# Attention and two dense layers fused on one core: the second layer's first three token blocks cut into two parts of four steps

## The chip, the core and the metric

The kernel runs on one core of one Trainium2 chip. The core has five engines with a queue of instructions each: PE (TensorE, matrix products; PEld is its weight load), DVE (VectorE), ACT (ScalarE), POOL (GpSimd) and SP (SyncE, which here only issues DMAs). An instruction waits for others by semaphores, and what stands behind it in its engine's queue waits with it. The metric is the device time of one execution in microseconds (us).

## The reference

```python
p_packed = sm_attn(p, k, v)              # 8 batches, 8 heads, 576 tokens, 32 packed queries
attn = sm_attn(q, p_packed, p_packed)    # -> x: 4608 tokens x 512
h = x @ w_in;   y = (h - tanh(h)) @ w_out        # layer 1, 512 -> 2048 -> 512
h = y @ w2_in;  out = (h * cos(h)) @ w2_out      # layer 2, the same sizes
```

All inputs are float64, the output is float32. The kernel keeps near float32 precision by splitting an operand into a high part (float32r) and the rest, and by summing three products of the parts.

## The kernel before, in words

**Weights.** `w2_in` and `w2_out` each come as 16 tiles of 128 x 512 in float64 words. A conversion (`Conv`) of one tile takes three stages: `a` is an ACT copy of the upper word, `b` are three DVE operations on the integer words (shift L144, sign L149, low bits L154), and `c` is an ACT copy to the high part (L177) with a POOL subtraction for the rest (L178). Each finished tile is also stored to memory for later reloading (`store_w2`). The order is w2_in 0, w2_out 0, w2_in 1, and so on; 32 conversions in all.

**Layer 1** runs 128 steps (16 half batches of tokens by 8 steps of 256 hidden units). During its last 16 steps, `STEP_A2` says how many conversions of layer 2 weights are begun in each; the three DVE operations of a conversion then stand between the five of the next step (`el2`).

**Layer 2** goes over nine blocks of 512 tokens. The first three (`NCL = 3`) are done directly, 8 steps each, 24 in all; they are numbered 0 to 23 here. One step s of such a block is: `h2` (24 matmuls, hidden units 256 s and on), `el_cos` and `chunks` of the step before (24 matmuls that add to the four y sums in PSUM). `el_cos` is a chain over two engines: round (ACT L599), fraction (DVE L602), sine and square (ACT L608, L609), product (DVE L612), high part gh (ACT L618), rest gl (DVE L621). PE needs gh of step n for `chunks` of step n, which stands behind `h2` of step n + 1. After a block's last step `evac` copies each of the four sums out and stores it.

In the first block each `el_cos` takes up to three conversions between its operations (`each("ca")`, `each("b")`). The next block's y comes in four pieces, `loady` (a DMA) and `splity` (ACT copy L565, POOL subtraction L566), one piece a step. In the third block two more things are prepared:

- `combine(F)` for F = 0 to 7 makes the weight sums that the later blocks use: two POOL operations on halves of w2_in tiles into `cw` (L670, L673), four POOL operations into `cs` (L681), then an ACT copy (`ws`, L683) and a DVE subtraction (`ws`, L684), and two stores. `COMBINE` gives the steps: 16, 16, 17, 17, 18, 18, 19, 20.
- `bprep` makes the y sums for the first pair of later blocks: 40 small pieces, loads of y (L736), DVE subtractions (L723, L730) and ACT copies (L720). It begins at the sixth step of the third block (`BPREP = 5`, step 21) and its pieces are spread evenly over the steps left.

**The other six blocks** are done in three pairs with fewer products (lines 1050 and on, matmuls L762), weights reloaded from memory. Their first products write PSUM that the direct blocks' h used, so they wait until the last step's product (L612) has read it.

**Order.** From step 15 of layer 1 on the order is that of the program text (`tc.manual_schedule`): every engine works its queue off in the order in which the code emits the instructions, and a pool slot is taken again in the order in which it was given back. Nothing reorders around a wait.

The steps of layer 2 before:

```python
h2(s, yt, st)
el_cos(st, t == 0, (t, s) == (0, 0))
...                       # splity, loady of the next block
    pend += chunks(ht, hs, hst)
...
store_w2()
if t == NCL - 1:
    for F in COMBINE[s]:
        combine(F)
```

Of the kernel before, what the change touches and what calls it, by code (L numbers as in the profile page):

```python
# [10 lines left out]
F32 = mybir.dt.float32  # L11
F32R = mybir.dt.float32r
# [22 lines left out]
PRE_A = (0, 1, 1, 1, 1, 0, 1, 1, 1, 0, 1, 1, 0, 0, 0)  # L35
PRE_B = (1, 0, 1, 1, 2, 0, 2, 2, 0, 1, 2, 2, 0, 3, 0)
STEP_A = (1, 2, 2, 2, 1, 2, 1, 1, 1, 1, 0, 2, 1, 1, 1, 1, 1, 1, 0, 3, 1, 1)
STEP_A2 = (1, 1, 1, 1, 1, 1, 1, 1, 1, 1, 1, 1, 1, 0, 0, 0)
STEP_ORDERED = 15
ATT1 = ((-2, 0, 1, 4), (0, 1, 2, 5))  # L40
ATT = ((0, 2, 3, 8), (1, 4, 5, 10))
# [2 lines left out]
PACK1, PACK = 3, 7  # L44
G0, G1, G = (0, 14, 12), (7, 8, 22, 25), (9, 11, 13, 15)
YLOAD, Y2LOAD, Y2SPLIT = 2, 118, 125
NCL, BPREP, COMBINE = 3, 5, ((0, 1), (2, 3), (4, 5), (6,), (7,), (), (), ())
SGN = -2147483648


# [1 line left out]
def fused_kernel(ctx, tc, qT, kT, v, pT, w1i, w1o, w2i, w2o, ident, out):  # L52
# [502 lines left out]
    def loady(t, k):  # L555
        yr = p2r.tile([128, TB], F32, tag="yr", bufs=2, name="yr")
        nc.sync.dma_start(out=yr, in_=y1[k, :, t * TB:t * TB + TB])
        return yr

    def splity(t, yr, eng):  # L560
        if t % 2 == 0:
# [23 lines left out]
        return p2.tile([128, 2, TB], dt, tag=tag, bufs=2, name=tag)  # L585

    def el_cos(st, cv, cut):
        def each(fns):
            if cv:
                for fn in fns:  # L590
                    getattr(conv2, fn)()

        h = st["h"]
        a = p2.tile([128, 2, TB], F32, tag="a", bufs=1, name="a")
        gh, gl = pt2("gh", F32R), pt2("gl", F32R)
        st["gh"], st["gl"] = gh, gl
# [3 lines left out]
        each("ca")  # L600
# [5 lines left out]
        each("b")  # L606
# [3 lines left out]
        each("ca")  # L610
# [5 lines left out]
        each("b")  # L616
        for x in parts:
            nc.scalar.activation(out=gh[:, x], in_=a[:, x], func=AF.Copy)  # L618
        each("ca")
# [4 lines left out]
        each("b")  # L624

    def chunks(t, s, st):
        def part(jobs):
            if s == 0 and t not in yps:
                yps[t] = [psy.tile([128, DM], F32, tag="y", name="y") for _ in range(4)]
            for m, lo in jobs:  # L630
                for x in range(2):
                    w = st["wo"][x]
                    for wh, gg in ((0, "gl"),) if lo else ((0, "gh"), (1, "gh")):
                        nc.tensor.matmul(  # L634
                            out=yps[t][m], lhsT=st[gg][:, x, 128 * m:128 * m + 128],
                            rhs=w[:, wh, :],
                            start=(s == 0 and x == 0 and not lo and wh == 0),
                            stop=(s == NSTEP - 1 and x == 1 and lo),
                        )
# [11 lines left out]
    def evac(t, m):  # L651
        if m < 2:
            o = p2.tile([128, DM], F32, tag="o", bufs=2, name="o")
        else:
            o = p2x["r"].tile([128, DM], F32, tag="wt", bufs=2, name="o")
        if m % 2 == 0:
            nc.scalar.activation(out=o, in_=yps[t][m], func=AF.Copy, scale=-TWO_PI)
        else:
            nc.vector.tensor_scalar(
                out=o, in0=yps[t][m], scalar1=-TWO_PI, scalar2=None, op0=ALU.mult  # L660
            )
# [343 lines left out]
    pend, hist, bo = [], [], {}
    for t in range(NCL):
        nyt = []
        for s in range(NSTEP):
            st = {}
            h2(s, yt, st)  # L1010
            el_cos(st, t == 0, (t, s) == (0, 0))
            if t + 1 < NCL:
                if 2 <= s < 6:
                    nyt.append(splity(t + 1, yr, nc.gpsimd))
                if 1 <= s < 5:
                    yr = loady(t + 1, s - 1)
            if hist:
                ht, hs, hst = hist.pop(0)
                conv2.need(w2out, 2 * hs + 1)
                hst["wo"] = [w2out[2 * hs + x] for x in range(2)]  # L1020
                pend += chunks(ht, hs, hst)
                n = 1 if (t, s) == (NCL - 1, NSTEP - 1) else len(pend)
                for fn in pend[:n]:
                    fn()
                pend = pend[n:]
            hist.append((t, s, st))
            store_w2()
            if t == NCL - 1:
                for F in COMBINE[s]:
                    combine(F)  # L1030
                if s == BPREP:
                    prep = bprep(NCL, bo)
                if s >= BPREP:
                    n = -(-len(prep) // (NSTEP - s))
                    for fn in prep[:n]:
                        fn()
                    prep = prep[n:]
        yt = nyt
# [162 lines left out]
```

## Time and profile before

| | us |
|---|---|
| median of 3 runs | 1578.78 (1578.52 to 1579.58) |
| the profiled execution | 1577.37 |
| its span, first to last instruction | 1575.5 |
| PE busy | 1491.6 (95%) |
| DVE busy | 1170.5 (74%) |
| ACT busy | 897.3 (57%) |
| POOL busy | 227.2 (14%) |

What lies outside the span is 1.9 us. In time, layer 1 ends at about 800 us of the span, the three direct blocks of layer 2 run from 800 to 1063 us, and the pairs from 1071 us to the end. PE's share of busy time is an average: the stretches in which it idles are few, and each has another cause. The profile's slices show PE at 8 tenths instead of 9 in the two slices before 788 us and at about 1063 us.

### The profile page before, as it was taken

What the parts mean: (1) busy time and instruction counts of PE and PEld (TensorE: products, weight loads), DVE (VectorE), ACT (ScalarE), POOL (GpSimd) and SP (SyncE); (2) the same over time, 40 slices, a digit from 0 to 9 for tenths busy, and PEclk for the clock granted to TensorE, in tenths of its full rate; (3) what the DMA queues carried; (4) which work ended last, traced back from release to release, by engine and by line L of the source; (5) the groups of instructions that cost most, each with busy time, mean ns of one, the idle gap of its engine ahead of it and who ended that gap; (6) DMA issues with size and microseconds to landing.
All of it is one profiled execution on the core that took longest, in us unless ns stands there. A gap on an engine that the chain in (4) does not pass through costs nothing.

```text
span 1575.5 us, 25882 instructions
## 1 busy us (share of the span) xinstructions
PE 1491.6 (95%) x10192; PEld 1293.6 (82%) x10192; DVE 1170.5 (74%) x1596; ACT 897.3 (57%) x1377; POOL 227.2 (14%) x178
## 2 busy tenths in 40 slices
PE   4789999999999999998899999998999999999999
PEld 1568888999999999998877788876888888888887
DVE  6999988787878788789979633567767477747661
ACT  4768655575666666667666543555555354535541
POOL 3632110010101010011314204720000000000000
PEclk9989999999999999999999999999999999999999
DMA  9422322111111111115647310426757474647542
GB/s 348 153 97 98 100 86 91 41 56 46 50 61 65 61 65 46 47 41 176 181 144 272 144 50 0 177 108 223 263 204 269 141 284 161 261 155 281 184 170 111
DMA packets 85050, 217.25 MB, mean 138 GB/s; under 512 B 8576, under 2 KB 36224, under 8 KB 84928
## 3 DMA queue, kind: packets, MB, share of 16 engines
q1 hardware_dynamic: 84928, 215.58, 38.9%
q8 instruction: 81, 1.33, 0.3%
q14 instruction: 41, 0.34, 0.1%
HBM read 169.15 MB, written 46.40 MB: 137 GB/s over the span
## 4 chain that ended last, share of the span: by engine, by line
PE 74%; DVE 15%; issue 4%; ACT 4%; POOL 2%; DMA 1%; SPq 0%; DVEq 0%; POOLq 0%; ACTq 0%
PE y L634 21%; PE y L513 20%; PE p L762 15%; PE h L451 10%; PE h L577 4%; DVE wt L144 2%; PE gp L413 2%; DVE wt L154 2%; DVE wt L149 2%; DVE y L481 1%; DVE t L478 1%; DVE d L479 1%; POOL cs L681 1%; PE pp L320 1%; DVE y L485 1%
## 5 line engine op out<-in xcount | busy, mean ns | idle before, releaser
L513 PE MATMUL y<-gh,w1o 128*128 128x288 f32 x2048 | 308.8, 302 | 16.9 <-ACT gh L493 11.9
L513 PEld LDWEIGHTS y<-gh,w1o 128*128 128x128 f32 x2048 | 281.6, 189 | 46.0 <-ACT t L466 14.9
L762 PE MATMUL p<-b,wa 128*128 128x512 f32 x1008 | 242.2, 391 | 7.6 <-DVE a L612 7.6
L451 PE MATMUL h<-a,g 128*128 128x288 f32 x1536 | 229.7, 299 | 14.6 <-ACT w1i L132 7.1
L451 PEld LDWEIGHTS h<-a,g 128*128 128x128 f32 x1536 | 214.1, 191 | 19.0 <-ACT w1i L132 8.0
L762 PEld LDWEIGHTS p<-b,wa 128*128 128x128 f32 x1008 | 190.5, 189 | 47.8 <-issue 8.0
L466 ACT ACTIVATE t<-h 128x576 f32<-128x576 f32 x128 | 83.3, 651 | 204.7 <-PE h L451 204.5
L634 PE MATMUL y<-wo,gh 128*128 128x512 f32 x768 | 188.1, 389 | 0.0
L634 PEld LDWEIGHTS y<-wo,gh 128*128 128x128 f32 x768 | 144.1, 188 | 30.0
L513 PE MATMUL y<-gl,w1o 128*128 128x288 f32 x1024 | 159.8, 298 | 1.2 <-DVE gl L498 1.2
L513 PEld LDWEIGHTS y<-gl,w1o 128*128 128x128 f32 x1024 | 144.9, 191 | 1.5 <-DVE gl L498 1.4
L577 PE MATMUL h<-yhl,w2i 128*128 128x512 f32 x576 | 134.3, 389 | 0.0
L478 DVE TENSOR_TENSOR t<-h,t 128x576 f32<-128x576 f32 x128 | 95.2, 744 | 52.4 <-ACT u L467 52.0
L485 DVE COPY_PREDICATED y<-k,t 128x576 f32<-128x576 int16 x128 | 118.4, 925 | 11.6
L577 PEld LDWEIGHTS h<-yhl,w2i 128*128 128x128 f32 x576 | 108.1, 188 | 22.4
L493 ACT ACTIVATE gh<-y 128x576 fp32r<-128x576 f32 x128 | 87.6, 684 | 37.5 <-DVE y L485 35.7
L498 DVE TENSOR_TENSOR gl<-y,gh 128x576 fp32r<-128x576 f32 x128 | 102.8, 803 | 6.8 <-ACT gh L493 6.6
L773 ACT ACTIVATE a<-ha 128x1024 f32<-128x1024 f32 x24 | 25.5, 1063 | 140.7 <-DVE ha L770 140.7
L634 PE MATMUL y<-w2o,gh 128*128 128x512 f32 x384 | 93.8, 392 | 8.2 <-ACT gh L618 8.2
L481 DVE SCALAR_TENSOR_TENSOR y<-y,d 128x576 f32<-128x576 f32 x128 | 101.4, 792 | 0.1
L634 PE MATMUL y<-wo,gl 128*128 128x512 f32 x384 | 97.8, 389 | 0.0
L479 DVE TENSOR_TENSOR d<-u,h 128x576 f32<-128x576 f32 x128 | 95.0, 742 | 0.0
(119 smaller groups left out, 2128.6 us busy)
## 6 DMA issues: line engine op xcount, KB each, us to landing
wo<-wod SPq DMA_DIRECT2D x96, 512.0 KB, 6.5
wa<-wsd SPq DMA_DIRECT2D x48, 512.0 KB, 6.2
wa<-wid SPq DMA_DIRECT2D x24, 512.0 KB, 5.5
y<-ye SPq DMA_DIRECT2D x80, 144.0 KB, 1.9
out<-o SPq DMA_DIRECT2D x36, 256.0 KB, 2.2
st<-w1i SPq DMA_DIRECT2D x16, 512.0 KB, 7.7
v<-vv SPq DMA_DIRECT2D x16, 512.0 KB, 4.6
st<-w1o SPq DMA_DIRECT2D x16, 512.0 KB, 6.5
```

Of the source, the lines that this page charges most:

```text
L451: nc.tensor.matmul(out=h[:, x, 0:HB], lhsT=gw[b, f // 4, half][:, ga, c0:c0 + 128], rhs=a2[b, half][:, aa, HB * j:HB * j + HB], start=(n = ...
L466: nc.scalar.activation(out=st["t"], in_=h, func=AF.Tanh)
L478: lambda: nc.vector.tensor_tensor(out=t, in0=hs, in1=t, op=ALU.subtract),
L479: lambda: nc.vector.tensor_tensor(out=d, in0=u, in1=hs, op=ALU.mult),
L481: lambda: nc.vector.scalar_tensor_tensor(out=y, in0=y, scalar=PC0 - PC1 * PC1 / (4 * PC2), in1=d, op0=ALU.add, op1=ALU.mult,),
L485: lambda: nc.vector.copy_predicated(out=y, mask=k.bitcast(I16), data=t),
L493: nc.scalar.activation(out=st["gh"], in_=st["g"], func=AF.Copy)
L498: nc.vector.tensor_tensor(out=st["gl"], in0=st["g"], in1=f32(st["gh"]), op=ALU.subtract)
L513: nc.tensor.matmul(out=yps[blk][d][:, 0:HB], lhsT=w1out[f][:, wh, 128 * d:128 * d + 128], rhs=st[gg][:, x, :], start=(s in first and x == ...
L577: nc.tensor.matmul(out=h[:, x, :], lhsT=w2in[f][:, wa, 128 * k:128 * k + 128], rhs=yt[k][:, ya, :], start=(n == 0), stop=(n == 11),)
L634: nc.tensor.matmul(out=yps[t][m], lhsT=st[gg][:, x, 128 * m:128 * m + 128], rhs=w[:, wh, :], start=(s == 0 and x == 0 and not lo and wh == 0),
L762: nc.tensor.matmul(out=dst, lhsT=wa[wi][:, 128 * j:128 * j + 128], rhs=b[j][:, bi, :], start=(n == 0), stop=(n == 5),)
```

## The change

- `PARTS` orders the 24 steps of the direct blocks anew: block 0 steps 0 to 3, block 1 steps 0 to 3, block 2 all eight, block 0 steps 4 to 7, block 1 steps 4 to 7. The sums of the first parts are stored to a new buffer in memory (`op`), loaded again (`load_op`) and added on DVE when the second part is copied out. y of blocks 0 and 1 is loaded and split twice.
- `el_cos` takes two conversions a step over steps 0 to 11 (`CONVS = 12`) instead of three over the first block; `STEP_A2` starts 10 conversions in layer 1 instead of 13.
- The pieces of y for the next part are loaded in pairs and split in pairs, in two steps: steps 1 and 2, 5 and 6, 13 and 14, 17 and 18.
- `combine` comes at steps 12, 13, 14, 15, 16, 16, 17, 17, and its results lie in slots of the weights' pool instead of the y pieces' pool.
- `bprep` begins at step 19 instead of 21, so its 40 pieces go 8 a step.

```diff
-STEP_A2 = (1, 1, 1, 1, 1, 1, 1, 1, 1, 1, 1, 1, 1, 0, 0, 0)
+STEP_A2 = (1, 1, 0, 1, 1, 0, 1, 1, 0, 1, 1, 0, 1, 1, 0, 0)
...
-NCL, BPREP, COMBINE = 3, 5, ((0, 1), (2, 3), (4, 5), (6,), (7,), (), (), ())
+PARTS = ((0, 0, 4), (1, 0, 4), (2, 0, 8), (0, 4, 8), (1, 4, 8))
+NCL, CONVS, BPREP = 3, 12, 19
+COMBINE = {12: (0,), 13: (1,), 14: (2,), 15: (3,), 16: (4, 5), 17: (6, 7)}
...
+    op = dram.tile([2, 4, 128, DM], F32, name="op")
...
     def el_cos(st, cv, cut):
-        def each(fns):
-            if cv:
+        def each(i, fns):
+            if i < cv:
                 for fn in fns:
                     getattr(conv2, fn)()
...
+    def load_op(t):
+        oparts[t] = []
+        for m in range(4):
+            o = otile(m)
+            nc.sync.dma_start(out=o, in_=op[t, m])
+            oparts[t].append(o)
+
+    def evac(t, m, lo_s, hi_s):
+        ps = yps[t, lo_s][m]
+        if lo_s:
+            o = oparts[t][m]
+            nc.vector.scalar_tensor_tensor(
+                out=o, in0=ps, scalar=-TWO_PI, in1=o, op0=ALU.mult, op1=ALU.add
+            )
         else:
...
-        nc.sync.dma_start(out=out[r0:r0 + 128, :], in_=o)
+        nc.sync.dma_start(out=out[r0:r0 + 128, :] if hi_s == NSTEP else op[t, m], in_=o)
...
-        hi, lo = (p3.tile([128, 4, 256], F32R, tag="yhl", bufs=4, name="ws") for _ in range(2))
+        hi, lo = (wp.tile([128, 4, 256], F32R, tag="w", name="ws") for _ in range(2))
...
+    for n, (i, t, s, a, b) in enumerate(seq):
+        st = {}
+        if s == a and i:
+            yt, nyt = nyt, []
+        h2(s, yt, st)
+        el_cos(st, 2 if n < CONVS else 0, n == 0)
+        if i < len(nxt):
+            r = s - a - (b - a - 4)
+            if r in (1, 2):
+                for _ in range(2):
+                    nyt.append(splity(i + 1, yr0.pop(0), nc.gpsimd))
+            if r in (0, 1):
+                yr0 += [loady(nxt[i], k) for k in range(2 * r, 2 * r + 2)]
+        if hist:
+            flush(*hist.pop(0))
...
+        if a and s == b - 2 and n < len(seq) - 2:
+            load_op(t)
+        store_w2()
+        for F in COMBINE.get(n, ()):
+            combine(F)
+        if n == BPREP:
+            prep = bprep(NCL, bo)
```

Where it moves instructions, first POOL in the third block. Here `yhl` is a split of a y piece, `cw` and `cs` are one combine. Before, all splits stand ahead of the first combine and none behind:

```order
L566 TENSOR_TENSOR yhl<-yr,yhl 128x512 x4
L670 TENSOR_TENSOR cw<-w2i 128x512
L673 TENSOR_TENSOR cw<-w2i 128x512
L681 TENSOR_TENSOR cs<-cw 128x256
L681 TENSOR_TENSOR cs<-cs,cw 128x256
L681 TENSOR_TENSOR cs<-cw 128x256
L681 TENSOR_TENSOR cs<-cw,cs 128x256
```

In the changed program, from the split of step 13 to the combine of step 14:

```order
L569 TENSOR_TENSOR yhl<-yr,yhl 128x512 x2
L691 TENSOR_TENSOR cw<-w2i 128x512
L694 TENSOR_TENSOR cw<-w2i 128x512
L702 TENSOR_TENSOR cs<-cw 128x256
L702 TENSOR_TENSOR cs<-cs,cw 128x256
L702 TENSOR_TENSOR cs<-cw 128x256
L702 TENSOR_TENSOR cs<-cw,cs 128x256
L569 TENSOR_TENSOR yhl<-yr,yhl 128x512 x2
L691 TENSOR_TENSOR cw<-w2i 128x512
```

The splits now stand between the combines, two ahead of the combine of step 13, two ahead of that of step 14, and two ahead of the two of step 17.

Second, ACT at the same place. Here `ws` is the copy that needs the end of a combine, and `a<-h` the round that begins the next step's chain. Before, from step 18's gh on:

```order
L618 ACTIVATE gh_11378<-a_11377 128x1024
L683 ACTIVATE ws_11419<-cs_11412 128x1024
L683 ACTIVATE ws_11433<-cs_11426 128x1024
L599 ACTIVATE a_11464<-h_11439 128x1024
L608 ACTIVATE a_11464<-a_11464 128x1024
```

In the changed program, from step 17's gh to step 18's:

```order
L621 ACTIVATE gh_11384<-a_11383 128x1024
L568 ACTIVATE yhl_11393<-yr_11290 128x512
L568 ACTIVATE yhl_11396<-yr_11292 128x512
L704 ACTIVATE ws_11439<-cs_11432 128x1024
L704 ACTIVATE ws_11453<-cs_11446 128x1024
L602 ACTIVATE a_11484<-h_11459 128x1024
L611 ACTIVATE a_11484<-a_11484 128x1024
L612 ACTIVATE a_11484<-a_11484 128x1024
L621 ACTIVATE gh_11485<-a_11484 128x1024
```

Both programs put the `ws` copies ahead of the next round; the changed one also has the ACT copies of the splits (`yhl`) behind gh and ahead of `ws`. Steps 13 and 14 read the same with one `ws` each.

Third, ACT at the last step of the direct blocks, where `b` are copies of `bprep`. Before, from step 22's gh to step 23's round:

```order
L618 ACTIVATE gh_11692<-a_11691 128x1024
L720 ACTIVATE b_11727<-yq_11646 128x512
L720 ACTIVATE b_11729<-yq_11646 128x512
L720 ACTIVATE b_11738<-yq_11733 128x512
L720 ACTIVATE b_11742<-yt_11737 128x512
L599 ACTIVATE a_11770<-h_11745 128x1024
```

In the changed program:

```order
L621 ACTIVATE gh_11785<-a_11784 128x1024
L741 ACTIVATE b_11819<-yt_11755 128x512
L741 ACTIVATE b_11823<-yt_11755 128x512
L741 ACTIVATE b_11827<-yq_11753 128x512
L602 ACTIVATE a_11854<-h_11829 128x1024
```

The copy from the freshly loaded second piece (`b_11738<-yq_11733` before) stood here one step ahead of the end; the changed program has its counterpart (`b_11756<-yq_11751`) one step earlier.

## Rows read from the trace of the kernel before

**Rows 1.** Windows: us; PE, PEld, DVE, ACT, POOL busy (count); clock, DMA share, GB/s.

```profile
700.00:720.00 20.00, 20.00 (x152) 20.00 (x151) 17.40 (x26) 14.61 (x27) 2.61 (x2) 1.00 0.34 110
740.00:760.00 20.00, 14.67 (x106) 13.93 (x105) 19.69 (x27) 13.68 (x26) 3.93 (x3) 1.00 0.58 190
860.00:880.00 20.00, 17.60 (x76) 14.29 (x77) 19.14 (x19) 11.63 (x16) 9.35 (x7) 1.00 0.84 317
```

**Rows 2.** Timeline of DVE, end of layer 1: start us, us, what [idle before].

```profile
731.72 0.74 DVE L478 TENSOR_TENSOR t<-h,t 128x576 f32<-128x576 f32 x1
...
737.94 0.74 DVE L478 TENSOR_TENSOR t<-h,t 128x576 f32<-128x576 f32 x1
...
789.05 0.74 DVE L478 TENSOR_TENSOR t<-h,t 128x576 f32<-128x576 f32 x1
...
792.62 0.74 DVE L478 TENSOR_TENSOR t<-h,t 128x576 f32<-128x576 f32 x1
```

**Rows 3.** Timeline of PE, first block of layer 2 and the step behind.

```profile
800.39 11.05 PE L577 MATMUL h<-yhl,w2i 128*128 128x512 f32 x48
...
873.57 3.92 PE L634 MATMUL y<-w2o,gh 128*128 128x512 f32 x16 [1.42 <-ACT gh L618]
...
879.15 5.60 PE L577 MATMUL h<-yhl,w2i 128*128 128x512 f32 x24
...
891.77 5.60 PE L577 MATMUL h<-yhl,w2i 128*128 128x512 f32 x24
...
902.65 5.60 PE L577 MATMUL h<-yhl,w2i 128*128 128x512 f32 x24
```

**Rows 4.** Groups of instructions, 812 to 885 us: count | busy us, mean ns | idle.

```profile
L144 DVE TENSOR_SCALAR wt<-wt 128x512 int32<-128x512 int32 x18 | 20.9, 1158 | 2.2
L149 DVE SCALAR_TENSOR_TENSOR wt<-st,wt 128x512 int32<-128x512 int32 x18 | 16.4, 912 | 0.6
L154 DVE SCALAR_TENSOR_TENSOR wt<-st,wt 128x512 int32<-128x512 int32 x18 | 12.5, 692 | 0.6
L602 DVE SCALAR_TENSOR_TENSOR a<-a,h 128x1024 f32<-128x1024 f32 x6 | 7.3, 1214 | 0.0
L566 POOL TENSOR_TENSOR yhl<-yr,yhl 128x512 fp32r<-128x512 f32 x4 | 6.0, 1493 | 0.0
```

**Rows 5.** Timeline of ACT, an undisturbed step's gh, and step 18 to 19.

```profile
903.16 1.06 ACT L618 ACTIVATE gh<-a 128x1024 fp32r<-128x1024 f32 x1 [1.29 <-DVE a L612]
...
1020.48 1.06 ACT L683 ACTIVATE ws<-cs 128x1024 fp32r<-128x1024 f32 x1 [5.00 <-POOL cs L681]
...
1027.51 1.06 ACT L618 ACTIVATE gh<-a 128x1024 fp32r<-128x1024 f32 x1 [1.29 <-DVE a L612]
```

**Rows 6.** Timeline of ACT, step 22 to 23, end of the direct blocks.

```profile
1063.86 0.63 ACT L720 ACTIVATE b<-yq 128x512 fp32r<-128x512 f32 x1 [3.05 <-DMA yq<-y]
...
1065.19 1.01 ACT L599 ACTIVATE a<-h 128x1024 f32<-128x1024 f32 x1
```

**Rows 7.** Timeline of PE, third block and the first products of the pairs.

```profile
1028.62 3.92 PE L634 MATMUL y<-w2o,gh 128*128 128x512 f32 x16 [0.69 <-ACT gh L618]
...
1061.39 1.97 PE L634 MATMUL y<-w2o,gh 128*128 128x512 f32 x8
1070.98 6.23 PE L762 MATMUL p<-b,wa 128*128 128x512 f32 x18 [7.62 <-DVE a L612]
```

**Rows 8.** Timeline of POOL, third block: a split, then combines.

```profile
959.22 1.83 POOL L566 TENSOR_TENSOR yhl<-yr,yhl 128x512 fp32r<-128x512 f32 x1 [9.05 <-ACT yhl L565]
961.00 1.29 POOL L670 TENSOR_TENSOR cw<-w2i 128x512 f32<-128x512 f32 x1
...
966.52 1.30 POOL L670 TENSOR_TENSOR cw<-w2i 128x512 f32<-128x512 f32 x1
...
1013.12 1.30 POOL L670 TENSOR_TENSOR cw<-w2i 128x512 f32<-128x512 f32 x1
...
1020.52 1.29 POOL L670 TENSOR_TENSOR cw<-w2i 128x512 f32<-128x512 f32 x1
```

More of the change, by code (lines that the diff above doesn't have):

```diff
@@ L558, in loady, with splity @@
         return yr
-    def splity(t, yr, eng):
-        if t % 2 == 0:
+    def splity(i, yr, eng):
+        if i % 2 == 0:
             t = a2p.tile([128, 2, S], F32R, tag="a2", bufs=4, name="yhl")[:, :, 0:TB]
@@ L599, in el_cos @@
             nc.scalar.activation(out=a[:, x], in_=h[:, x], func=AF.Identity, bias=MAGIC)
-        each("ca")
+        each(0, "ca")
         for x in parts:
@@ L605, in el_cos @@
             )
-        each("b")
+        each(0, "b")
         for x in parts:
@@ L609, in el_cos @@
             nc.scalar.activation(out=a[:, x], in_=a[:, x], func=AF.Square, scale=SQRT2)
-        each("ca")
+        each(1, "ca")
         for x in parts:
@@ L615, in el_cos @@
             )
-        each("b")
+        each(1, "b")
         for x in parts:
             nc.scalar.activation(out=gh[:, x], in_=a[:, x], func=AF.Copy)
-        each("ca")
+        each(2, "ca")
         for x in parts:
@@ L623, in el_cos, with chunks @@
             )
-        each("b")
-    def chunks(t, s, st):
+        each(2, "b")
+    def chunks(t, s, st, lo_s=0, hi_s=8):
         def part(jobs):
-            if s == 0 and t not in yps:
-                yps[t] = [psy.tile([128, DM], F32, tag="y", name="y") for _ in range(4)]
+            if s == lo_s and (t, lo_s) not in yps:
+                yps[t, lo_s] = [psy.tile([128, DM], F32, tag="y", name="y") for _ in range(4)]
             for m, lo in jobs:
@@ L634, in part @@
                         nc.tensor.matmul(
-                            out=yps[t][m], lhsT=st[gg][:, x, 128 * m:128 * m + 128],
+                            out=yps[t, lo_s][m], lhsT=st[gg][:, x, 128 * m:128 * m + 128],
                             rhs=w[:, wh, :],
-                            start=(s == 0 and x == 0 and not lo and wh == 0),
-                            stop=(s == NSTEP - 1 and x == 1 and lo),
-                        )
-                if s == NSTEP - 1 and lo:
-                    evac(t, m)
-        if s == NSTEP - 1:
+                            start=(s == lo_s and x == 0 and not lo and wh == 0),
+                            stop=(s == hi_s - 1 and x == 1 and lo),
+                        )
+                if s == hi_s - 1 and lo:
+                    evac(t, m, lo_s, hi_s)
+        if s == hi_s - 1:
             groups = [[(m, False), (m, True)] for m in range(4)]
@@ L649, in chunks, with otile @@
         return [lambda g=g: part(g) for g in groups]
-    def evac(t, m):
+    oparts = {}
+    def otile(m):
         if m < 2:
-            o = p2.tile([128, DM], F32, tag="o", bufs=2, name="o")
-        else:
[L655 to L661, printed above, removed]
+            return p2.tile([128, DM], F32, tag="o", bufs=2, name="o")
+        return p2x["r"].tile([128, DM], F32, tag="wt", bufs=2, name="o")
+    def load_op(t):
[11 more added lines that the diff above has]
+            )
+        else:
+            o = otile(m)
+            if m % 2 == 0:
+                nc.scalar.activation(out=o, in_=ps, func=AF.Copy, scale=-TWO_PI)
+            else:
+                nc.vector.tensor_scalar(
+                    out=o, in0=ps, scalar1=-TWO_PI, scalar2=None, op0=ALU.mult
+                )
         r0 = t * TB + 128 * m
-        nc.sync.dma_start(out=out[r0:r0 + 128, :], in_=o)
+        nc.sync.dma_start(out=out[r0:r0 + 128, :] if hi_s == NSTEP else op[t, m], in_=o)
     def combine(F):
@@ L1004, in fused_kernel @@
     p3c, p3 = run_pool("p3")
[L1005 to L1038, printed above, removed]
@@ new lines, in fused_kernel, with flush @@
+    pend, hist, bo, nyt = [], [], {}, []
+    seq = [(i, t, s, a, b) for i, (t, a, b) in enumerate(PARTS) for s in range(a, b)]
+    nxt = [p[0] for p in PARTS[1:]]
+    def flush(ht, hs, hst, a, b):
+        conv2.need(w2out, 2 * hs + 1)
+        hst["wo"] = [w2out[2 * hs + x] for x in range(2)]
+        pend.extend(chunks(ht, hs, hst, a, b))
+    for n, (i, t, s, a, b) in enumerate(seq):
[13 more added lines that the diff above has]
+            flush(*hist.pop(0))
+            keep = 2 if n == len(seq) - 1 else 0
+            while len(pend) > keep:
+                pend.pop(0)()
+        hist.append((t, s, st, a, b))
+        if a and s == b - 2 and n < len(seq) - 2:
[5 more added lines that the diff above has]
+            prep = bprep(NCL, bo)
+        if n >= BPREP:
+            m = -(-len(prep) // (len(seq) - n))
+            for fn in prep[:m]:
+                fn()
+            prep = prep[m:]
@@ L1039, in fused_kernel @@
     was = [load_wa(0)]
-    ht, hs, hst = hist.pop(0)
-    hst["wo"] = [w2out[2 * hs + x] for x in range(2)]
-    pend += chunks(ht, hs, hst)
+    flush(*hist.pop(0))
     p3c.__exit__(None, None, None)
@@ L1049, in fused_kernel @@
     p4 = p2x["r"]
+    load_op(PARTS[-1][0])
     def p4t(tag, bufs=2):
```

## The prediction

> **What bounds the kernel now.** I read the windows first, in 20 us pieces. PE does its matmuls without a gap in most of them; three stretches lose time. At 740 us, in the last 16 steps of layer 1, DVE is busy 19.69 of 20 us and PE makes 106 matmuls where it made 152 at 700 us [rows 1]. At 860 us, in layer 2's first block, DVE is busy 19.14 us and PE waits again. Both are the stretches in which weights are converted. Then I read the engines' timelines for what each step costs. A layer 1 step with a conversion takes DVE 6.22 us (731.72 to 737.94), one without 3.57 (789.05 to 792.62) [rows 2]; PE needs 36 matmuls, 36 x 20/152 = 4.7 us [rows 1]. In layer 2 a step without conversions takes 10.88 us (891.77 to 902.65), one with three 12.62 (879.15 to 891.77), and the reader sees PE stop for ACT's gh [rows 3]. The last stretch is the change to the pairs, where PE idles until the last step's product is done.
>
> **Part 1, three conversions less in layer 1.** 15 steps remain behind the first. Before, 13 with a conversion: 13 x 6.22 + 2 x 3.57 = 88.0. After, 10: 10 x 6.22 + 5 x 3.57 = 80.1, still above PE's 15 x 4.7 = 71, so DVE goes on setting the pace: 7.9 us less. If four of the light steps, now between heavy ones, had to wait for PE (4.7 instead of 3.57), 4.5 of it would go: 3.4 left. The two light steps that the trace shows ran at 3.57 without a gap, so I take 7.0.
>
> **Part 2, two conversions a step instead of three in layer 2.** From 800.39 to 902.65 there are 9 groups of h and 8 of y matmuls, each 10.88 / 2 = 5.44 us: 92.5 of 102.3 us, 9.8 lost [rows 3]. A conversion on DVE takes 1.16 + 0.91 + 0.69 = 2.76 us, the chain's three operations 1.21 each [rows 4]. Three conversions and the chain make 11.9 us, over PE's 10.88 and DVE-bound with its small waits; two make 9.2, under it. So the waits of steps 1 to 7 go and the first one stays: 9.0. Against it: at steps 4 and 8 the part's last sum is copied out into a slot that a conversion still holds until ACT and POOL have done the next step's first conversion; that DVE copy, and the fraction behind it, come some 3 us late. gh has 3.9 us to spare (its copy ends at 904.22 [rows 5], its matmuls start at 902.65 + 5.44 = 908.09 [rows 3]), so it is covered, barely. I take 8.5, bounds 6 and 9.
>
> **Part 3, bprep begun two steps sooner.** In step 22 ACT stood on a copy that waited 3.05 us for the second y load, and the last step's round started only at 1065.19 [rows 6], 3.8 us behind the end of its h matmuls at 1061.4 [rows 7]. The load can now start when step 20's pieces have freed its buffers and is needed in step 21, so the round starts on time: PE's idle time falls from 7.62 [rows 7] to 3.8 us. What is late next is the chain itself, 5.8 us from round to product (1065.19 to 1070.98), less 1.8 us of y matmuls. Behind the gap 18 products took 6.23 us, where 18 x 5.44 / 24 = 4.08 is the full pace; a shorter gap may spare that 2.15 or not, I take half. Together 4.8, bounds 3.8 and 6.0.
>
> **Part 4, the combines.** The old wait of step 18 to 19 goes: 0.69 us idle [rows 7] and about 0.3 to refill (as 12.62 - 10.88 = 1.74 stands to 1.42 idle [rows 3]), 1.0. But new ones come. In the changed queues POOL has, at step 13, two y splits and then the combine; the splits need ACT's copies, which stand behind gh. ACT has next the ws copy, which needs the combine, and behind it the round of step 14. Everything of step 14's chain is queued behind that copy, on ACT and so on DVE, and PE's y matmuls wait for its gh. From one gh to the next this path takes:
> - ACT's copy until POOL can start: 0.6, and two splits. The split behind gh took 1.78 us to the next start (959.22 to 961.00 [rows 8]) with DVE's gl beside it, the mean is 1.49 [rows 4]: 3.3.
> - a combine: 5.52 (961.00 to 966.52), or 7.40 with DVE beside it (1013.12 to 1020.52 [rows 8]). DVE has nothing to do while ACT waits, so 5.5.
> - ws to the end of the next gh: 1020.48 to 1028.57 [rows 5], 8.1.
>
> That is 17.5 where PE's step takes 10.88: 6.6 late. Step 14's gh has 3.9 to spare, so PE waits 2.8; step 14 does the same with nothing to spare, 6.6 more. Step 15 has a combine but no split, and POOL runs it ahead; step 16's two also. By step 17 gh has regained 0.5 to 3.2, I take 1.9. There the splits stand ahead of two combines: 0.6 + 3.3 + 5.5 + 6.4 (the second beside a DVE subtraction, between 5.52 and 7.40) + 8.1 = 23.9, 13.0 late, 11.1 of waiting. Sum 20.5, and 3 x 0.3 refill: 21.4.
>
> Two of these gaps are near the 7.62 us gap or above it, after which the products ran slow. A slow restart behind each: 2 x 2.15 = 4.3. Part 4 costs 25.7. Bounds: splits at 1.49, 3.2 regained and no slow restart 18.5; combines at 7.40 and three slow restarts 37.
>
> The Trainium skill, "SBUF — State Buffer" (section "SBUF: two separate sides"), says that a DVE operation with two SBUF inputs and a GpSimd operation lock each other out for a whole instruction. The trace agrees: combines took 5.52 to 7.40 us. By that rule the combines run at 5.5 while DVE stands still; at 7.40 throughout, part 4 would cost about 6 more. Its "TensorE: Matmul & The Clock Gate" (section "HAM oscillation — how this bites in real kernels") says that an idle array falls back to half clock and pays for it at each return. The 6.23 us behind the one long gap agree; by it the new waits cost more than their idle time, and without it part 4 would cost 21.4.
>
> **Costed at nothing.** Eight more y pieces: their four in steps 1 to 6 lie on ACT and POOL beside 10.88 us steps, those of steps 13 to 18 are in part 4. Eight stores and eight loads of part sums, 256 KB each, lie on SP and the DMA queues ahead of their use by a step or more. Sixteen copies out become eight plus eight DVE additions of the same size. If that cover fails it is one copy's wait each, some 1 us. PE's matmuls are the same in number and shape.
>
> **Sum.** Gains 7.0 + 8.5 + 4.8 + 1.0 = 21.3 (14 to 24), cost 25.7 (18.5 to 37): 4.4 us slower. Against the profiled execution, 1577.4 (span 1575.5 and 1.9 around it), that is 1581.8; the median of the runs is 1.4 above that execution, so 1583.2.
>
> **Rivals.**
> - *PE restarts at full pace behind the new gaps.* Then part 4 costs 21.4 and the change comes to nothing: 0.1 slower, 1578.9. For it: PE restarted at once behind the small waits [rows 3]. Against it: the one gap as long as these was followed by 6.23 us for 4.08 [rows 7].
> - *POOL does not hold the rounds up* (faster). Place: the ws copies of steps 13, 14 and 17. If the path from gh to gh is no longer than 13 us instead of 17.5, steps 13 and 14 cost nothing (3.9 to spare, 2.1 lost each), and by the same 4.5 us less step 17 costs under 7; if it is shorter still, only the gains remain: about 21 less, 1557.5, and 1567 with step 17's wait and one slow restart. It decides once part 4 costs under 18. For it: the slack hid most of POOL's lateness before, 5.00 us of ACT waiting cost PE 0.69 idle ([rows 5, 7]). Against it: then POOL had no split behind gh in its queue, and ran ahead.
> - *Combines as slow as under load, or layer 1 held by its light steps*: some 6 or 4 more, 10 for both, 1593. For it: 7.40 was measured in the very steps of the combines [rows 8]; against it, DVE is idle in the waits.
>
> **Chances.** Forecast 0.48 (own range 1577.5 to 1588.5), full pace 0.14, POOL no hindrance 0.16, the slow case 0.22. About 0.2%, 3.2 us, is what a measurement can tell from no change. Forecast: 0.33 slower, 0.14 the same, 0.01 faster; full pace 0.12 the same, 0.02 faster; POOL no hindrance 0.16 faster; slow case 0.20 slower, 0.02 the same. Faster 0.19, same 0.28, slower 0.53. The range 1570 to 1592 leaves out most of the third case and the ends of the others.
>
> **What would show it.** Layer 1's last steps: fewer steps of 6.2 us on DVE, end of layer 1 some 7 us sooner. First blocks: steps of 10.88 with PE not waiting for gh behind step 0. Steps 13 to 18: PE gaps released by ACT's gh of about 3, 7 and 11 us, ACT's ws copies waiting for POOL, POOL's splits waiting for ACT. Change to the pairs: a gap of about 4 us. The forecast is wrong if the gaps of steps 14, 15 and 18 are missing or under 15 us together, or if DVE in the last layer 1 steps does not set the pace any more.

## The result, and the profile after

The changed kernel takes 1588.25 us (median of 4 runs, 1587.21 to 1591.49) where the kernel before took 1579.0 on the same chip: ratio 1.0062, 95% interval 1.0044 to 1.0079, so 9.3 us slower. The forecast was 1583.2, 4.4 slower. The profiled execution has a span of 1586.1 us, 10.6 more than before. All line numbers from here on are the changed kernel's, three higher up to the y matmuls and some twenty behind them; some experiments shift them again by a few. A step's y matmuls stand behind the next step's h2.

Followed along PE's timeline, the 10.6 us are made up like this. Stretches are bounded by the starts of h2 groups and products.

| stretch | before | after | difference | forecast |
|---|---|---|---|---|
| start to first h2 (layer 1) | 800.39 | 795.39 | -5.0 | -7.0 |
| first h2 to step 10 | 113.14 | 111.42 | -1.7 | -8.5 |
| waits of the combines, new | 0 | 22.2 | +22.2 | +25.7 |
| old wait of step 18 to 19 | 1.0 | 0 | -1.0 | -1.0 |
| last h2 to first products, and these | 21.3 | 17.5 | -3.8 | -4.8 |
| sum | | | +10.7 | +4.4 |

**Layer 1** answers to [rows 2]. DVE's timeline, in the last steps of layer 1 of the changed kernel: start, duration, instruction, idle before it and who ended that.

```profile
734.99 0.74 DVE L481 TENSOR_TENSOR t<-h,t 128x576 f32<-128x576 f32 x1
...
738.63 0.76 DVE L481 TENSOR_TENSOR t<-h,t 128x576 f32<-128x576 f32 x1
...
744.88 0.75 DVE L481 TENSOR_TENSOR t<-h,t 128x576 f32<-128x576 f32 x1
...
755.93 0.76 DVE L481 TENSOR_TENSOR t<-h,t 128x576 f32<-128x576 f32 x1 [1.16 <-ACT u L470]
...
761.81 0.76 DVE L481 TENSOR_TENSOR t<-h,t 128x576 f32<-128x576 f32 x1 [0.67 <-ACT u L470]
```

A light step is 3.64 us (734.99 to 738.63), a heavy one 6.25 (738.63 to 744.88), as before. But at 756 and 762 DVE waits for ACT's u, 1.83 us together, which nothing made it do before: there PE is behind. PE's row says why.

```profile
753.97 3.91 PE L516 MATMUL y<-gh,w1o 128*128 128x288 f32 x16 [3.08 <-ACT ye L552]
```

In the kernel before the same row stands:

```profile
759.48 3.06 PE L513 MATMUL y<-gh,w1o 128*128 128x288 f32 x16 [3.11 <-ACT ye L549]
```

In the middle of the 16 steps PE has to wait some 3 us for ACT to empty the y banks. Behind DVE at 6.2 us a step it caught up unseen; now DVE has to wait for it in two steps.

**First steps of layer 2**, answering to [rows 3]: PE's timeline, with rows in which PE waits.

```profile
795.39 11.05 PE L580 MATMUL h<-yhl,w2i 128*128 128x512 f32 x48
...
827.45 1.20 PE L580 MATMUL h<-yhl,w2i 128*128 128x512 f32 x4 [0.59 <-ACT w2i L180]
...
857.53 1.20 PE L637 MATMUL y<-w2o,gh 128*128 128x512 f32 x4 [1.02 <-DVE o L680]
...
889.92 0.73 PE L637 MATMUL y<-w2o,gl 128*128 128x512 f32 x2 [1.20 <-DVE gl L624]
...
903.95 1.20 PE L637 MATMUL y<-w2o,gh 128*128 128x512 f32 x4 [1.02 <-DVE o L680]
...
906.81 5.60 PE L580 MATMUL h<-yhl,w2i 128*128 128x512 f32 x24
```

The waits for gh behind step 0 are gone, as forecast, and others stand in their place: for late weights, for gl, and for the copies of the first parts' sums. DVE's timeline over steps 1 to 5 shows where it loses the time; below it are ACT's round of step 2 and POOL's split of step 1.

```profile
811.35 1.22 DVE L605 SCALAR_TENSOR_TENSOR a<-a,h 128x1024 f32<-128x1024 f32 x1 [1.15 <-ACT a L602]
...
818.05 1.67 DVE L157 SCALAR_TENSOR_TENSOR wt<-st,wt 128x512 int32<-128x512 int32 x1
819.65 2.32 DVE L624 TENSOR_TENSOR gl<-a,gh 128x1024 fp32r<-128x1024 f32 x1
823.13 1.22 DVE L605 SCALAR_TENSOR_TENSOR a<-a,h 128x1024 f32<-128x1024 f32 x1 [1.15 <-ACT a L602]
...
834.90 1.22 DVE L605 SCALAR_TENSOR_TENSOR a<-a,h 128x1024 f32<-128x1024 f32 x1 [1.15 <-ACT a L602]
...
844.58 1.22 DVE L605 SCALAR_TENSOR_TENSOR a<-a,h 128x1024 f32<-128x1024 f32 x1 [1.15 <-ACT a L602]
...
856.78 0.69 DVE L680 TENSOR_SCALAR o<-y 128x512 f32<-128x512 f32 x1 [3.08 <-POOL w2o L181]
857.39 1.21 DVE L605 SCALAR_TENSOR_TENSOR a<-a,h 128x1024 f32<-128x1024 f32 x1
```

```profile
822.07 1.03 ACT L602 ACTIVATE a<-h 128x1024 f32<-128x1024 f32 x1 [3.85 <-DVE gl L624]
```

```profile
817.78 3.12 POOL L569 TENSOR_TENSOR yhl<-yr,yhl 128x512 fp32r<-128x512 f32 x2 [0.77 <-ACT yhl L568]
```

From fraction to fraction (L605) DVE needs 9.68 us in a step with two conversions and no split (834.90 to 844.58), 11.78 in one with a split on POOL (811.35 to 823.13), and 12.81 where the copy of a sum waits for a slot (844.58 to 857.39); the last two are above PE's 10.88. Each fraction waits 1.15 us for ACT's round, because there is one tile a: the round of a step can't be written before gl of the step ahead has read it (ACT's round stood 3.85 us for gl), so DVE's whole work of a step and ACT's round form a closed loop. And beside the split, which POOL ran from 817.78 to 820.90, two DVE operations took 1.67 and 2.32 us where they take 0.69 and 1.22 otherwise: 2.08 us more, the difference between 9.68 and 11.78. The Trainium skill, "SBUF — State Buffer" (section "SBUF: two separate sides"), says that such operations of DVE and GpSimd lock each other out; these rows agree.

**The combines**, answering to [rows 5] and [rows 8]. First PE's timeline, the three gaps; then ACT's, then POOL's.

```profile
969.16 5.53 PE L637 MATMUL y<-w2o,gh 128*128 128x512 f32 x16 [2.35 <-ACT gh L621]
...
986.35 2.05 PE L637 MATMUL y<-w2o,gh 128*128 128x512 f32 x4 [4.40 <-ACT gh L621]
...
1030.51 5.65 PE L637 MATMUL y<-w2o,gh 128*128 128x512 f32 x16 [9.40 <-ACT gh L621]
```

```profile
950.85 1.06 ACT L621 ACTIVATE gh<-a 128x1024 fp32r<-128x1024 f32 x1 [1.29 <-DVE a L615]
951.81 1.14 ACT L568 ACTIVATE yhl<-yr 128x512 fp32r<-128x512 f32 x2
961.13 1.06 ACT L704 ACTIVATE ws<-cs 128x1024 fp32r<-128x1024 f32 x1 [8.18 <-POOL cs L702]
962.10 1.00 ACT L602 ACTIVATE a<-h 128x1024 f32<-128x1024 f32 x1
...
968.05 1.06 ACT L621 ACTIVATE gh<-a 128x1024 fp32r<-128x1024 f32 x1 [1.28 <-DVE a L615]
```

```profile
952.50 3.09 POOL L569 TENSOR_TENSOR yhl<-yr,yhl 128x512 fp32r<-128x512 f32 x2 [19.74 <-ACT yhl L568]
955.55 1.29 POOL L691 TENSOR_TENSOR cw<-w2i 128x512 f32<-128x512 f32 x1
...
960.36 0.74 POOL L702 TENSOR_TENSOR cs<-cw,cs 128x256 f32<-128x256 f32 x1
```

The reader sees the ring: ACT ends the copies for the split, POOL splits (3.1 us) and combines (5.5), ACT stands 8.18 us on the ws copy, and the round of the next step, one row further in ACT's queue, starts at 962.10 although its h was ready. From gh to gh it is 17.20 us (950.85 to 968.05); the forecast had 17.5. Steps 14 and 17 do the same; at step 17 two combines make it 23.69 (the copies to gh start at 1005.71 and 1029.40).

**Change to the pairs**, answering to [rows 7]: PE's timeline.

```profile
1081.96 5.95 PE L783 MATMUL p<-b,wa 128*128 128x512 f32 x18 [4.10 <-issue]
```

The profile names no releaser here ("issue"), but DVE's product of step 23, for which these matmuls waited in the kernel before, ends at 1081.86, 0.1 us ahead of them:

```profile
1080.64 1.22 DVE L615 SCALAR_TENSOR_TENSOR a<-a,h 128x1024 f32<-128x1024 f32 x1 [2.21 <-ACT a L612]
```

### The profile page after: what moved, and what is told of

It is laid out like the page before. It is cut to its first block, busy times and chain, and to the rows that moved or that the text cites. A ratio compares the mean times of both kernels' runs of the same rounds, so it can differ in the third digit from the quotient of the medians.

```text
span 1586.1 us, 25956 instructions
## 1 busy us (share of the span) xinstructions
PE 1497.8 (94%) x10192; PEld 1298.0 (82%) x10192; DVE 1171.5 (74%) x1604; ACT 900.2 (57%) x1385; POOL 234.5 (15%) x186
## 4 chain that ended last, share of the span: by engine, by line
PE 68%; DVE 16%; issue 8%; POOL 4%; ACT 3%; DMA 1%; SPq 0%; DVEq 0%; POOLq 0%; ACTq 0%
PE y L516 19%; PE y L637 19%; PE p L783 15%; PE h L454 9%; DVE wt L147 2%; PE h L580 2%; DVE y L484 2%; DVE wt L157 2%; PE gp L416 2%; DVE y L488 1%; POOL cs L702 1%; DVE d L482 1%; DVE wt L152 1%; DVE t L481 1%; DVE gl L501 1%
## 5 line engine op out<-in xcount | busy, mean ns | idle before, releaser
L516 PE MATMUL y<-gh,w1o 128*128 128x288 f32 x2048 | 310.5, 304 | 11.6 <-ACT gh L496 6.7
L637 PE MATMUL y<-wo,gh 128*128 128x512 f32 x768 | 188.1, 389 | 0.0
L637 PEld LDWEIGHTS y<-wo,gh 128*128 128x128 f32 x768 | 144.2, 188 | 29.9
L580 PEld LDWEIGHTS h<-yhl,w2i 128*128 128x128 f32 x576 | 108.0, 188 | 23.9 <-ACT w2i L180 1.0
L488 DVE COPY_PREDICATED y<-k,t 128x576 f32<-128x576 int16 x128 | 116.1, 907 | 11.6
L637 PE MATMUL y<-w2o,gh 128*128 128x512 f32 x384 | 99.1, 405 | 18.8 <-ACT gh L621 16.7
L637 PEld LDWEIGHTS y<-w2o,gh 128*128 128x128 f32 x384 | 74.7, 196 | 37.3 <-ACT gh L621 18.7
L637 PE MATMUL y<-wo,gl 128*128 128x512 f32 x384 | 97.8, 389 | 0.0
```

Source lines behind the costliest of these rows:

```text
L488: lambda: nc.vector.copy_predicated(out=y, mask=k.bitcast(I16), data=t),
L516: nc.tensor.matmul(out=yps[blk][d][:, 0:HB], lhsT=w1out[f][:, wh, 128 * d:128 * d + 128], rhs=st[gg][:, x, :], start=(s in first and x == ...
L580: nc.tensor.matmul(out=h[:, x, :], lhsT=w2in[f][:, wa, 128 * k:128 * k + 128], rhs=yt[k][:, ya, :], start=(n == 0), stop=(n == 11),)
L637: nc.tensor.matmul(out=yps[t, lo_s][m], lhsT=st[gg][:, x, 128 * m:128 * m + 128], rhs=w[:, wh, :], start=(s == lo_s and x == 0 and not lo ...
```

## The experiments

Times are medians; the kernel before stood at 1578.0 to 1579.0 beside them. Each edit is made on the changed kernel, or on the first three together where that is said. The last column is the difference to the changed kernel, or to edit 5.

| edit | us | ratio to before, 95% interval | against |
|---|---|---|---|
| changed kernel | 1588.25 | 1.0062 (1.0044 to 1.0079) | |
| 1 late splits on DVE | 1567.26 | 0.9925 (0.9908 to 0.9941) | -21.0 |
| 2 second tile a | 1585.39 | 1.0041 (1.0026 to 1.0056) | -2.9 |
| 3 other slot for sums | 1584.89 | 1.0039 (1.0025 to 1.0054) | -3.4 |
| 4 13 conversions in layer 1 | 1594.28 | 1.0098 (1.0083 to 1.0113) | +6.0 |
| 5 edits 1, 2, 3 | 1559.88 | 0.9882 (0.9867 to 0.9896) | -28.4 |
| 6 ws a step later | 1568.30 | 0.9936 (0.9919 to 0.9953) | -20.0 |
| 7 three conversions a step | 1604.42 | 1.0162 (1.0146 to 1.0177) | +16.2 |
| 8 edits 6, 2, 3 | 1562.28 | 0.9894 (0.9879 to 0.9908) | -26.0 |
| 9 edits 1, 2, 3 and 7 | 1574.49 | 0.9983 (0.9973 to 0.9992) | +14.6 on 5 |
| 10 edits 1, 2, 3, sums late | 1563.86 | 0.9903 (0.9887 to 0.9920) | +4.0 on 5 |

**1. The splits of steps 13 to 18 on DVE.**

```diff
-nyt.append(splity(i + 1, yr0.pop(0), nc.gpsimd))
+nyt.append(splity(i + 1, yr0.pop(0), nc.gpsimd if n < CONVS else nc.vector))
```

> The changed kernel with one edit: the y splits of steps 13, 14, 17 and 18 are subtracted on DVE instead of POOL, so that no split stands ahead of a combine in POOL's queue. Theory A (the 22.2 us that PE lost at steps 14, 15 and 18 come from the path gh, split, combine, ws copy, next round): POOL runs the combines ahead again, the three PE gaps go, and the time falls by 18 to 22 us to 1566 to 1570. Rival B (the eight combines are simply too much work for those six steps, whatever they stand behind, or the ws copies on ACT and DVE are): the gaps stay within a few us, 1583 to 1588. Rival C (DVE, with eight more subtractions of 0.69 us, becomes the next wait): some 5 us of new PE waits on DVE, 1571 to 1575.

Measured 1567.26: theory A. PE's waits from the first h2 to the last direct step, by releaser (us in total, times, longest):

```profile
PE y L637 <- DVE o L680: 2.0, 2, 1.0
PE y L637 <- DVE gl L624: 2.0, 2, 1.2
PE y L637 <- ACT gh L621: 0.6, 1, 0.6
...
```

Of 16.7 us of waiting for gh, 0.6 is left, and every step from 10 on takes 10.88. What is left belongs to steps 2 to 9.

**2. A second tile a in the odd steps before 10.**

```diff
-        a = p2.tile([128, 2, TB], F32, tag="a", bufs=1, name="a")
+        if alt:
+            a = wp.tile([128, 2, TB], F32, tag="w", name="a")
+        else:
+            a = p2.tile([128, 2, TB], F32, tag="a", bufs=1, name="a")
```

> The changed kernel with a second buffer for the chain's tile a in odd steps up to 9 (taken from the weights' pool, where slots are free then). Theory A (in steps 1 to 8 the loop over gl, round and fraction through the single buffer sets the pace: 11.8 us from fraction to fraction where the splits lie, 1.15 of it DVE idle for the round): the idle time goes, these steps take PE's 10.9, and 2 to 4 us of the 7.1 lost there come back: 1584 to 1586. Rival B (DVE's own work, slowed by POOL at the shared port, sets the pace): DVE gets fuller and PE waits the same, within 1 us of 1588.

**3. The first parts' sums of rows 2 and 3 in a tile of the conversions' output pool, not in a wt slot.**

```diff
-            o = otile(m)
+            if m < 2 or hi_s == NSTEP:
+                o = otile(m)
+            else:
+                o = wp.tile([128, 2, 512], F32, tag="w", name="o")[:, 0, :]
```

> The changed kernel with the third and fourth sum of a first part copied out into a free slot of the weights' pool instead of the slot that a conversion holds. Theory A (the 3.08 us in which DVE stood for POOL at steps 4 and 8, which I had costed at nothing, costs PE 1.0 us of idle twice and shifts the steps behind): both waits go and 2 to 3 us come back, 1585 to 1586. Rival B (the slack of gh covers it as forecast, and PE's 1.02 us come from DVE being late anyway): no difference beyond 0.5 us, 1588.

PE's waits in the same stretch, first of edit 2 (L640 is L637 there, L683 is L680), then of edit 3:

```profile
PE y L640 <- ACT gh L624: 16.1, 4, 8.9
PE y L640 <- DVE o L683: 2.0, 2, 1.0
```

```profile
PE y L637 <- ACT gh L621: 16.2, 4, 8.8
PE y L637 <- DVE gl L624: 1.3, 2, 0.8
...
```

Edit 2 takes 1585.39 us, inside theory A's range, edit 3 takes 1584.89, 0.1 us below it; single runs of edit 2 lie 3 us apart. Each takes away its own wait. With a second a, all steps run at 10.88 but 5 and 9, behind the copies, which take 12.2; with the other slot all from 5 on run at 10.88, and 2, 3 and 4 take 11.3 to 12.2. Steps 2 to 9 lose 2.6 and 2.9 us instead of 7.1. The two gains, 4.5 and 4.2, make more than 7.1 together, so they overlap: with the other slot steps 5 and 6 run at 10.88 although the loop still takes 11.8 there (fractions at 854.94, 866.72 and 878.51). Two long loops in a row are covered as long as nothing else is late.

**4. Part 1 undone.**

```diff
-STEP_A2 = (1, 1, 0, 1, 1, 0, 1, 1, 0, 1, 1, 0, 1, 1, 0, 0)
+STEP_A2 = (1, 1, 1, 1, 1, 1, 1, 1, 1, 1, 1, 1, 1, 0, 0, 0)
```

> The changed kernel with one part undone: 13 conversions are begun in layer 1 as before, so layer 2's first steps have 19 left instead of 22. Theory A (the lighter layer 1 steps are worth the 5.0 us by which layer 1 ended sooner, and the conversions left end two steps sooner): layer 1 ends 5 us later, and up to 1.5 us come back in steps 3 to 10, where the wait for w2_in of step 3 goes: 1591 to 1593. Rival B (conversions moved out of layer 1 only move the wait into layer 2's first steps): within 1.5 us of 1588.

1594.28, 6.0 us slower and 1.3 us above theory A's range; rival B is out. First h2 at 800.91 as in the kernel before, and only 0.7 us came back in the first steps of layer 2 (110.76 instead of 111.42 from the first h2 to step 10). Part 1 is worth 5 to 6 us. A single trace gives it no better than that, since the first h2 starts between 795.3 and 798.1 in the profiled executions of kernels whose layer 1 is the changed one.

**5 to 8.** The combination of edits 1, 2 and 3; the combines with their copies a step later; part 2 undone; and edit 6 with 2 and 3. The edits of 6 and 7:

```diff
         store_w2()
+        for F in list(cs):
+            combine_ws(F)
         for F in COMBINE.get(n, ()):
             combine(F)
```

Here combine keeps POOL's six additions, and combine_ws holds what followed them (ACT's copy, DVE's difference, two stores).

```diff
-        el_cos(st, 2 if n < CONVS else 0, n == 0)
+        el_cos(st, 3 if n < 8 else 0, n == 0)
```

> Three edits of the runs before it together: splits of y from step 12 on by DVE, a second buffer for the tile a in the odd steps before 10, and the first-part sums of rows 2 and 3 in tiles of another pool than wt. Theory A (the two losses lie one behind the other: 21 us in the queues of POOL and ACT around the combines, 7.1 us in steps 2 to 10 by the single a and by the o tiles that stand in the ring of wt): steps 2 to 10 take 8 x 10.88 = 87.0 instead of 94.1 us, so 1567.3 - 7.1 = 1560.2 us, within 1558.5 to 1562. Theory B (two conversions and a split in one step are more than DVE can do in 10.88, and the second buffer and the other tiles only shifted the wait): no more than one of the two gains of about 3 us, 1563.5 to 1567.

Edit 5: PE's waits from the first h2 to the first product, two of which are left.

```profile
PE p L789 <- issue: 4.1, 1, 4.1
PE y L640 <- ACT gh L624: 0.6, 1, 0.6
```

1559.88 us, as theory A had it (1560.2), and 19 us faster than the kernel before. From the first h2 to step 10 it takes 104.33 us (795.39 to 899.72) where the kernel before took 113.14: 8.8 us less, close to the 8.5 that the prediction gave part 2.

> The splits stay on POOL; of each combine only POOL's additions stay in their step, and ACT's copy and DVE's difference (ws) are issued one step later, so that ACT's copy no longer stands in ACT's queue ahead of the next step while POOL still works. Theory A (the loss is ACT waiting in its in-order queue for POOL): the three gaps of 4.3, 6.5 and 11.4 us on PE go, 1588.3 - 21 = 1567 us, within 1565 to 1570. Theory B (POOL's work is itself in the way, by its share of DVE's time or because the splits come late for the parts that need them): at most half of it comes back, 1576 to 1588.

Edit 6: 1568.30, theory A. POOL still does the same splits and combines; ACT's queue no longer stands on them. So it is the place of the copy in ACT's queue that cost 20 us, not POOL's work. ACT's timeline at the same steps:

```profile
950.39 1.06 ACT L621 ACTIVATE gh<-a 128x1024 fp32r<-128x1024 f32 x1 [1.29 <-DVE a L615]
951.35 1.14 ACT L568 ACTIVATE yhl<-yr 128x512 fp32r<-128x512 f32 x2
952.40 1.05 ACT L710 ACTIVATE ws<-cs 128x1024 fp32r<-128x1024 f32 x1
955.51 1.03 ACT L602 ACTIVATE a<-h 128x1024 f32<-128x1024 f32 x1 [2.07 <-PE h L580]
```

> Undoes part 2 alone: three conversions in each of steps 0 to 7 of layer 2 instead of two in each of steps 0 to 11. By the prediction part 2 is worth 8.5 us, so 1588.3 + 8.5 = 1596.8 us. By the traces (step 10 of layer 2 came 6.7 us sooner, of which 5.0 are layer 1) it is worth 1.7 us: 1590 us, within 1588 to 1592, with steps of about 12 us up to step 7 and 10.88 behind it.

Edit 7: 1604.42, neither expectation held. In this kernel part 2 is worth nearly twice the 8.5 us that the prediction gave it, not a fifth. Windows from h2 of step 2 to h2 of step 8, in the kernel before, the changed one and this one (length; busy time and count of PE, PEld, DVE, ACT, POOL; clock, DMA share, GB/s):

```profile
817.67:891.77 74.10, 67.14 (x290) 53.60 (x289) 66.66 (x68) 47.92 (x63) 29.20 (x21) 1.00 0.69 249
```

```profile
812.69:882.21 69.52, 66.86 (x290) 53.62 (x288) 57.15 (x56) 43.38 (x58) 28.61 (x21) 1.00 0.68 227
```

```profile
814.45:898.55 84.10, 71.50 (x289) 55.56 (x288) 74.61 (x75) 50.70 (x70) 37.46 (x26) 0.96 0.76 272
```

The six steps take 12.4, 11.6 and 14.0 us in the mean, and DVE is busy 90%, 82% and 89% of them. With three conversions a step, the stretch from the first h2 to step 10 is 12.2 us longer than it was before (125.4 against 113.1). Two a step give back 14.0. So the 1.7 us gained in the changed kernel are the difference of two large terms. The 12.2 us are not the parts of four steps alone: edit 7 keeps part 1, so 22 conversions lie in this stretch instead of 19, and three of them are 8.5 us of DVE's time (1.09 + 0.87 + 0.87 us each there).

> The late ws of the run before the last, the second a buffer and the first-part sums in tiles of another pool, splits on POOL throughout. Theory A: as the first run of this set, 1558.5 to 1562 us, since the 21 us and the 7.1 us are both gone. Theory B: 1565 us or more, since the split of 3.1 us on POOL and the combine behind it still take turns with DVE.

Edit 8: 1562.28, 0.3 us above theory A's range and far from theory B's 1565, 2.4 us behind edit 5: the two ws copies of step 18 still keep PE waiting 0.95 us, and the products wait 4.80 instead of 4.10.

**9. Part 2 undone where the other waits are gone.** Edits 1, 2 and 3 with edit 7, the second a in steps 1, 3 and 5 alone. With it in steps 7 and 9 as well, the same kernel deadlocks and has no time.

> The three edits together (1559.9 us), the second a buffer in steps 1, 3 and 5 alone, and part 2 undone: three conversions in each of steps 0 to 7 instead of two in each of steps 0 to 11. Theory A (part 2 alone is worth the 8.5 us of the prediction, and the 16 us that undoing it cost in the changed kernel contain the waits for a, wt and the splits on top): 1559.9 + 8.5 = 1568.4 us, within 1566 to 1571, steps 2 to 7 of about 12.3 us. Theory B (the splits and copies that parts of four steps bring into steps 1 to 8 fill DVE whatever the tiles, so that two per step save what they saved in the changed kernel): 1559.9 + 16.2 = 1576 us, within 1573 to 1579, with single steps of 13 us and more.

1574.49, 14.6 us over edit 5, in theory B's range (single runs from 1573.5 to 1578.6). The second a and the other slot help at three conversions a step too: the stretch from the first h2 to step 10 is 120.03 us (795.32 to 915.35), 5.4 less than in edit 7. But they don't bring its steps to 10.88: DVE is now busy 95% (69.43 of 73.00 us from 812 on), and PE's timeline has gaps of 2.4 us in steps 3 and 4. The 6.9 us that the stretch is longer than before hold three more conversions here as well, so how much of them the splits and copies cost, as theory B has it, is not shown.

```profile
832.67 3.94 PE L640 MATMUL y<-w2o,gh 128*128 128x512 f32 x16 [2.39 <-ACT gh L624]
...
846.21 2.08 PE L640 MATMUL y<-w2o,gh 128*128 128x512 f32 x4 [2.35 <-ACT gh L624]
```

**10. Part 3 undone, on edits 1, 2 and 3.**

```diff
-NCL, CONVS, BPREP = 3, 12, 19
+NCL, CONVS, BPREP = 3, 12, 21
```

> The three edits together, with part 3 undone: the y sums of the first pair begin at step 21 instead of step 19. Theory A (as the traces show it, 15.0 instead of 11.5 us between the last h2 and the first product, and 0.3 in the product itself): 1559.9 + 3.8 = 1563.7 us, within 1562.5 to 1565.5. Theory B (the first product waits for DVE's product of step 23 in any case, so sooner sums buy nothing): 1559 to 1561 us.

1563.86, theory A. The wait is back as it was in [rows 7]:

```profile
1058.11 6.61 PE L789 MATMUL p<-b,wa 128*128 128x512 f32 x18 [7.67 <-DVE a L618]
```

## Why the prediction came out as it did

The direction and the cause that decides it were right, and the time lay inside the range, 5 us over the forecast. By the prediction's own sign the forecast stands, since the three gaps make 16.2 us, over 15; that DVE sets the pace in layer 1's last steps failed in two of them. The sum of 4.4 against 10.7 is made of one step that failed and three terms of another size. That it came so close is in part luck: gains of 9.8 us less than forecast (6.8 of them in part 2) were met by a cost 3.5 us smaller, and the time lies at the upper end of the forecast's own range (1577.5 to 1588.5).

- **Failed: "Costed at nothing", and with it part 2's "covered, barely".** The prediction said of four of the eight more y pieces that they "lie on ACT and POOL beside 10.88 us steps", and that DVE's late copy at steps 4 and 8 is hidden. Neither holds. A split on POOL stretches two DVE operations by 2.1 us in its step, and the copy waits 3.08 us for its slot with the next fraction behind it. The 9.2 us that two conversions leave on DVE are under 10.88, but the loop through the one tile a also holds ACT's round and the waits around it, and with the split's 2.1 us it comes to 11.78. Taking a second a and another slot (edits 2, 3 and 5) brings these steps to 10.88 and the stretch to -8.8: part 2's 8.5 was the right size for what it counted. The reasoning checked gh against its 3.9 us of slack and did not look at what else a late DVE holds up: gl, the round that needs gl, and PE's next sums, which wait for the copy itself (1.02 us, twice; the 1 us that it named for a cover that fails). Edits 7 and 9 show what two conversions a step instead of three are worth once these pieces are there: 14 to 16 us.
- **Part 1, 7.0, measured 5 to 6.** The steps cost what the forecast took. It missed PE's wait of 3 us for the emptied y banks, which a slower DVE had hidden; behind it DVE waited for PE in two steps and lost 1.83. The bound of 3.4 named such waits, in four light steps.
- **Part 4, 25.7, measured 22.2.** The path from gh to gh was right (17.2 for 17.5; 23.7 for 23.9 at step 17), and edits 1 and 6 show by two ways that it is the cause: 21.0 and 20.0 us come back. Idle time was 2.35 + 4.40 + 9.40 = 16.2, forecast 20.5; what the gaps cost beyond it was 6.1, forecast 5.2. The sum had added up two things that overlap. Behind the first gap PE ran slowly and was itself late, so the second wait was shorter by as much: the first two gaps cost 10.8 us, and 2 x 6.3 of lateness less the 3.9 to spare and one slow restart of 2.0 is 10.7. And by step 17 gh had regained 3.3 us (its copy ends at 1006.77, its matmuls start at 1010.07) instead of the 1.9 taken. The bounds, 18.5 and 37, don't follow from the terms named for them, which give some 19 and 34.5; the 22.2 lies between either pair.
- **Part 3, 4.8, measured 3.8 to 4.0** (trace, and edit 10). Half of the slow restart was booked as spared; 5.95 instead of 6.23 us for the 18 products spares 0.3, and edits 5 and 10 don't show even that (6.82 us behind a gap of 4.10, 6.61 behind 7.67). The idle time fell to 4.10, forecast 3.8.
- **Old wait, 1.0:** gone.
- **Rivals.** PE does not restart at full pace: 16 matmuls took 5.53 and 5.65 us behind the gaps, 3.79 elsewhere. POOL is a hindrance. The slow case was half right on layer 1 (5 to 6 us, between 7.0 and 3.4), and its price for the combines was not: 5.5 us each while ACT stood, 6.5 for the second of step 17, where the forecast had 6.4.

Open is how much of the 12.2 us in edit 7 is the splits, how much the copies and how much the three more conversions; no run parts them.

## What to carry to other kernels

An instruction that waits for another engine belongs behind the next step's urgent work in its own in-order queue; 20 us came back by issuing eight copies, with the differences behind them, one step later. When work is moved beside a chain that seems to have slack, follow every operand of the next step round its buffers, single tiles above all, not only the one result that PE waits for. A slow restart and the wait behind it are not to be added: the time that PE loses in one is taken from the other.

## What the runs showed of the hardware

Windows of the changed kernel from PE's first matmul behind the 2.35 and the 9.40 us gap, and of ones before and behind; the third number from the end is the granted clock, as a share of the higher level.

```profile
960.00:966.00 6.00, 6.00 (x29) 4.95 (x28) 2.36 (x2) 3.32 (x4) 1.10 (x2) 1.00 0.43 175
969.20:974.70 5.50, 5.50 (x17) 4.38 (x18) 1.17 (x1) 0.95 (x2) 4.99 (x4) 0.69 0.00 0
...
1030.60:1036.00 5.40, 5.40 (x17) 4.28 (x18) 2.33 (x2) 3.77 (x5) 3.06 (x2) 0.67 0.55 208
1037.00:1047.00 10.00, 10.00 (x46) 8.29 (x45) 5.38 (x7) 4.38 (x6) 0.00 (x0) 1.00 0.00 0
```

The granted clock is 1.00 ahead of the gaps, 0.69 and 0.67 in the 5.5 us behind them, so for a part of these at the lower level (1.2 of 2.4 GHz), and 1.00 again later. A gap of 2.35 us cost nearly as much of this as one of 9.40 (16 matmuls in 5.53 and 5.65 us), which I had not expected. Length alone does not decide it: in edit 9 a gap of 2.39 us was followed by 16 matmuls in 3.94 us at a granted clock of 1.00, and one of 2.35 by four in 2.08 at 0.50, the lower level.
